# SwiGLU feed-forward on one core: gate and up of three chunks computed together, weights loaded once for three matmul pairs

## The chip, the core and the metric

The kernel runs on 1 core of one Trainium2 chip. The metric is the device time of one execution in microseconds (us), lower is better. A time before or after is the median of several runs. The profile comes from one execution by itself, whose own time is given beside its span.

## The reference

```python
def reference(x, w_gate, w_up, w_down):
    g = _silu(x @ w_gate)
    u = x @ w_up
    return (g * u) @ w_down
```

x is 1 x 2048 x 512, w_gate and w_up are 512 x 1376, w_down is 1376 x 512, all bfloat16. Two matrix products of the same input (gate and up), SiLU of the first, their product element by element, and a third matrix product (down).

## The kernel before, in words

The 2048 rows of x (tokens) are cut into 4 chunks of 512 (SC). The kernel holds x transposed (xT_sb: the 512 features on partitions, in 4 steps dk of 128), all weights, and the hidden values (hT_sb) in on-chip memory. A matmul takes a weight tile as its stationary operand (lhsT) and 512 tokens as its moving operand (rhs), and adds up the four steps dk in one of 8 banks of 128 x 512 float32.

**Groups.** One group is what fills one bank. The list `groups` fixes the order of PE's work and the bank of each group (number of the group modulo 8). For each chunk c and each of ten tiles ft of 128 hidden columns there is a group "G" (gate) and a group "U" (up), planned by `plan_pair`. 1376 is 10 x 128 + 96; the last 96 columns are handled apart: group "X" of a chunk (`plan_x`) holds the last 96 gate columns and the last 32 up columns, and group "Y" (`plan_y`) holds 64 further up columns for two chunks at once. The order is: for chunk 0 its ten G, U pairs, then X; the same for chunks 1, 2 and 3; then Y of chunks 0 and 1, Y of chunks 2 and 3. Then follow the groups "O" of the down product.

**Who reads a bank.** ACT (the scalar engine) computes SiLU of a G bank into one of NSG = 4 buffers sg_sb; DVE (the vector engine) multiplies it with the U bank into hT_sb. Of an X bank ACT takes two SiLUs (into sgx_sb and sgy_sb) and DVE one product (hx_sb). Of a Y bank DVE takes one product with sgy_sb (hy_sb). The operations stand in two lists, act_ops and dve_ops, in the order of planning, and each engine works its list in that order, waiting on semaphores: s_P counts finished groups, s_A and s_D the finished operations of ACT and DVE.

**What PE waits for.** Before a group's first matmul `free(g)` (L327) waits until all readers of the group eight places earlier, which had the same bank, are through. `gu_needs` (L348) waits for the loads: x of the chunk (x1, x2 or x3, for chunk 0 parts of its own) and the slab of weights. A load is waited for once. All waits are on PE's own instruction stream, so everything behind a wait waits too.

**Pairs.** From the fifth group on (`in_pairs`), `whole` (L334) issues each step dk as two matmuls of 64 weight columns each, at column 0 and column 64 of the array, writing the lower and the upper half of the same bank with the same moving operand. Each matmul brings its own weight load, which the profile shows as LDWEIGHTS on PEld.

**The loads.** SP issues nearly all DMAs in a written-out order (`loads_on_sync`, L124): parts of x of chunk 0 and the weights first, then the transposing loads x1, x2, x3 (L136, issued in L95), then w_down.

**The down product.** After the last Y group PE waits for all hT_sb. Then `strips` (L447) works in quads: four O groups at once, one for each chunk, each matmul using 32 rows of the array, with four row positions side by side (L470). The first pass works quad 0 and then quad 1, each over all ten tiles, before any other strip; `strips` calls `free` for all four groups of a quad before its first matmul. Quad 0 takes the banks of the groups eight to five places before the first O group, quad 1 those of the last four groups before it. In the kernel before, these last four are U of the last tile of chunk 3, X of chunk 3, and the two Y. The last four token tiles end with whole matmuls (L506). ACT and DVE copy the O banks to o_sb, and SP (one of the last by ACT) stores them.

Of the kernel before, what the change touches and what calls it, by code (L numbers as in the profile page):

```python
# [14 lines left out]
def bass_standalone__swiglu_ffn__prompt_kernel(nc, x, w_gate, w_up, w_down, out):  # L15
    _, S, D = x.shape
    F = w_gate.shape[1]
    P = 128
    KD = D // P
    NFF = F // P  # L20
    NFT = NFF + 1
    F_LAST = F - NFF * P
    SC = 512
    NSC = S // SC
# [5 lines left out]
    HT = SC // 2  # L30
    NXN = HT // P
    NB = 8
    NSG = 4
    NOS = 8
    SR = 32
    PW = 64
# [2 lines left out]
    Y_ROWS = [0, 64, 0, 64]  # L39
    X_ROWS = [64, 0, 96, 32]  # L40
    ORDER = [1, 2, 3, 0]
    assert D == 512 and S % SC == 0 and KD == 4 and F_LAST == 96 and NSC % 2 == 0

    xf = x[0]
# [3 lines left out]
    UPH = F + 32  # L48
    WTOT = 2 * F
    XC0 = NFF * P  # L50
    YC0 = UPH + NFF * P

    with ExitStack() as es:
# [7 lines left out]
        hT_sb = sb("hT_sb", [P, NFF, S], BF16)  # L61
# [3 lines left out]
        adummy = sb("act_dummy", [P, 8], FP32)  # L65
        sg_sb = [sb(f"sg_sb{i}", [P, SC], FP32) for i in range(NSG)]
        sgx_sb = [sb(f"sgx_sb{c}", [P, SC], FP32) for c in range(NSC)]
# [10 lines left out]
        s_P = sem("s_P")  # L78
# [70 lines left out]
        groups = []  # L149
# [3 lines left out]
        def add_group(kind, **what):  # L153
            g = dict(kind=kind, at=len(groups), bank=banks[len(groups) % NB], readers=[], **what)
            groups.append(g)
            return g

        def add_op(eng, g, **what):
            n_read[eng] += 1
            op = dict(g=g, at=n_read[eng], **what)  # L160
            (act_ops if eng == "A" else dve_ops).append(op)
            g["readers"].append((eng, op["at"]))
            return op

        def tview(i, dk):
            return banks[KD * i + dk][:, 0:P // 2].bitcast(BF16)

        sg_reader = []
        n_sg = 0
        h_ready = {}  # L170

        def plan_pair(c, ft):
            nonlocal n_sg
            gg = add_group("G", c=c, ft=ft)
            gu = add_group("U", c=c, ft=ft)
            b = n_sg % NSG
            free = sg_reader[n_sg - NSG] if n_sg >= NSG else 0
            a = add_op("A", gg, kind="silu", out=sg_sb[b][:, :], src=gg["bank"][:, :], free=free)
            d = add_op(
                "D", gu, kind="mul", out=hT_sb[:, ft, c * SC:(c + 1) * SC], a=sg_sb[b][:, :],  # L180
                b=gu["bank"][:, :], after=a["at"],
            )
            sg_reader.append(d["at"])
            h_ready[c] = d["at"]
            n_sg += 1

        def yblk(c):
            return (0, 64) if c % 2 == 0 else (64, 128)
# [4 lines left out]
        def plan_x(c):  # L193
            g = add_group("X", c=c)
            y0, y1 = yblk(c)
            add_op("A", g, kind="silu", out=sgx_sb[c][96:128, :], src=g["bank"][64:96, :], free=0)
            a = add_op("A", g, kind="silu", out=sgy_sb[c // 2][y0:y1, :], src=g["bank"][0:64, :], free=0)
            d = add_op(
                "D", g, kind="mul", out=hx_sb[X_ROWS[c]:X_ROWS[c] + SR, c, :],
                a=sgx_sb[c][96:128, :], b=g["bank"][96:128, :], after=a["at"] - 1,  # L200
            )
            y_after[c // 2] = a["at"]
            t_ready[c] = d["at"]
# [10 lines left out]
        for i in range(NXN):  # L214
            for dk in range(KD):
# [3 lines left out]
                    out=xT_sb[:, dk, i * P:(i + 1) * P], src=tview(i, dk), stored=(None, 0),  # L219
                )  # L220
                xt_ready[i, dk] = (eng, op["at"])

        for c in range(NSC):
            for ft in range(NFF):
                plan_pair(c, ft)
            plan_x(c)
        for pi in range(NSC // 2):
            plan_y(pi)
# [3 lines left out]
        n_store = [0] * NOS  # L232
        tiles = [c * TPC + q for q in range(TPC) for c in ORDER]
        for at, t in enumerate(tiles):
            ob = at % NOS
            if at == 2 * TPC:
                parted = add_op(
                    "D", dict(readers=[]), kind="copy", ready=(s_T, N_TURNS), out=part_sb[:, :],
                    src=banks[(NO + NST - 1) % NB][:, LASTH:D], stored=(None, 0),
# [4 lines left out]
            for c0, c1 in parts:  # L244
                g = add_group("O", t=t, c0=c0, c1=c1)
# [66 lines left out]
        def on_tensor(pe):  # L312
            landed = set()

            def need(name, count=1):
                if name not in landed:
                    pe.wait_ge(loads[name], 16 * count)
                    landed.add(name)
# [3 lines left out]
            def after(eng, n):  # L322
                if n > read[eng]:
                    pe.wait_ge(s_A if eng == "A" else s_D, n)
                    read[eng] = n

            def free(g):  # L327
                if g["at"] >= NB:
                    for eng, n in groups[g["at"] - NB]["readers"]:
                        after(eng, n)  # L330

            in_pairs = False

            def whole(bank, dk, col, c, n0, n1):  # L334
                if not in_pairs:
                    return pe.matmul(  # L336
                        bank[:, n0:n1], lhsT=w_sb[:, dk, col:col + P],
                        rhs=xT_sb[:, dk, c * SC + n0:c * SC + n1], start=(dk == 0), stop=(dk == KD - 1),
                    )
                for y0 in (0, PW):  # L340
                    ins = pe.matmul(  # L341
                        bank[y0:y0 + PW, n0:n1], lhsT=w_sb[:, dk, col + y0:col + y0 + PW],
                        rhs=xT_sb[:, dk, c * SC + n0:c * SC + n1], start=(dk == 0), stop=(dk == KD - 1),
                        tile_position=(0, y0), skip_group_check=True,
                    )
                return ins

            def gu_needs(g, n0, n1):  # L348
                c, ft = g["c"], g["ft"]
                if c > 0:  # L350
                    need(f"x{c}")
                if c == 0 and n1 > HT:
                    need("x0b")
                if c == 0 and n1 > HT + P:
                    need("x0c")
                need(("wg" if g["kind"] == "G" else "wu") + str(slab_of[ft]))

            def gu_step(g, dk, n0, n1):
                c = g["c"]
                col = (0 if g["kind"] == "G" else UPH) + g["ft"] * P  # L360
                if c == 0:
                    for i in range(n0 // P, min(n1 // P, NXN)):
                        after(*xt_ready[i, dk])
                ins = whole(g["bank"], dk, col, c, n0, n1)
                if n1 == SC and dk == KD - 1:
                    ins.then_inc(s_P, 1)

            def gu_matmuls(g, n0, n1):
                if g["c"] == 0:
                    for i in range(n0 // P, min(n1 // P, NXN)):  # L370
                        after(*xt_ready[i, 0])
                gu_needs(g, n0, n1)
                for dk in range(KD):
                    gu_step(g, dk, n0, n1)
# [38 lines left out]
                gu_matmuls(g, HT, SC)  # L413

            for g in groups[NB:NO]:
                free(g)
                kind = g["kind"]
                if kind in "GU":
                    gu_matmuls(g, 0, SC)
                elif kind == "X":  # L420
                    c = g["c"]
                    need(f"wg{slab_of[NFF]}")
                    need("wut")
                    for dk in range(KD):
                        ins = whole(g["bank"], dk, XC0, c, 0, SC)
                    ins.then_inc(s_P, 1)
                elif kind == "Y":
                    need(f"wu{slab_of[NFF]}")
                    for dk in range(KD):
                        for c in (2 * g["pi"], 2 * g["pi"] + 1):  # L430
                            y0, y1 = yblk(c)
                            ins = pe.matmul(  # L432
                                g["bank"][y0:y1, :], lhsT=w_sb[:, dk, YC0:YC0 + 64],
                                rhs=xT_sb[:, dk, c * SC:(c + 1) * SC],
                                start=(dk == 0), stop=(dk == KD - 1),
                                tile_position=(0, y0), skip_group_check=True,
                            )
                    ins.then_inc(s_P, 1)
# [8 lines left out]
            def strips(q, k, fks, start, stop, turn=True):  # L447
# [7 lines left out]
                for fk in fks:  # L455
                    if fk == NFF:
                        need("wdt", 2 + TPC)
                    for c, g in zip(ORDER, quad):
                        t = g["t"]
# [38 lines left out]
            for g in groups[NO + TPC * (TPC - 1):]:  # L498
# [6 lines left out]
                for fk in full[1:]:  # L505
                    ins = pe.matmul(  # L506
                        g["bank"][:, 0:c1 - c0], lhsT=hT_sb[:, fk, t * P:(t + 1) * P],
                        rhs=wd_sb[:, fk, c0:c1], start=(rest and fk == 1), stop=(fk == NFF - 1),
                        skip_group_check=True,
                    )  # L510
# [3 lines left out]
        on_gpsimd(nc.gpsimd)  # L514
        on_scalar(nc.scalar)
        on_tensor(nc.tensor)
        on_vector(nc.vector)

# [27 lines left out]
```

## Time and profile before

| | |
|---|---|
| time, median of 3 runs | 120.16 us |
| the runs | 119.78 to 120.52 us |
| the profiled execution's own time | 120.42 us |
| its span, first to last instruction | 119.1 us |
| PE busy | 116.2 us, 98% |
| PE weight loads (PEld) busy | 63.5 us, 1386 loads |
| DVE busy / ACT busy | 38.8 us / 35.1 us |
| granted TensorE clock | 1.000 |

How to read it: PE is the matmul engine, PEld its weight loads, which can run beside a matmul, and SP the queue that issues most DMAs. A group of instructions in the profile is named by line, engine and operation, "out<-in" by the program's tile names and the shapes (partitions x elements), then the count, the busy time in us and the mean duration of one in ns, then the idle time of the engine just before them and what ended it. A row of the timeline gives start and length in us, then the engine, the line and the merged instructions with their count. Matmuls of one engine overlap in part: a matmul's own duration is longer than the time from its start to the start of the next, so the rate is read from a row of many.

### The profile page before, as it was taken

What the parts mean: (1) busy time and instruction counts of PE and PEld (TensorE: products, weight loads), DVE (VectorE), ACT (ScalarE), POOL (GpSimd) and SP (SyncE); (2) the same over time, 40 slices, a digit from 0 to 9 for tenths busy, and PEclk for the clock granted to TensorE, in tenths of its full rate; (3) what the DMA queues carried; (4) which work ended last, traced back from release to release, by engine and by line L of the source; (5) the groups of instructions that cost most, each with busy time, mean ns of one, the idle gap of its engine ahead of it and who ended that gap; (6) DMA issues with size and microseconds to landing.
All of it is one profiled execution on the core that took longest, in us unless ns stands there. A gap on an engine that the chain in (4) does not pass through costs nothing.

```text
span 119.1 us, 3076 instructions
## 1 busy us (share of the span) xinstructions
PE 116.2 (98%) x1385; PEld 63.5 (53%) x1386; DVE 38.8 (33%) x62; ACT 35.1 (29%) x62; POOL 0.5 (0%) x5
## 2 busy tenths in 40 slices
PE   7999999999999999999999999999999999999993
PEld 2999555555555555555555555544444444444463
DVE  0204634444334444344353344361000044004322
ACT  3406443262442363432454423430000033002121
POOL 1000000000000000000000000000000000000000
DMA  4999989995000000000000000000000015300522
GB/s 92 281 197 336 262 175 99 263 331 155 6 0 0 0 6 0 0 3 3 6 0 0 0 0 6 0 0 0 6 0 6 0 47 196 115 6 0 194 76 88
DMA packets 17533, 8.78 MB, mean 74 GB/s; under 512 B 10608, under 2 KB 17520, under 8 KB 17520
## 3 DMA queue, kind: packets, MB, share of 16 engines
q1 hardware_dynamic: 16704, 8.23, 28.9%
q10 hardware_dynamic: 816, 0.36, 1.1%
q8 instruction: 11, 0.18, 0.6%
q14 instruction: 2, 0.02, 0.0%
HBM read 4.65 MB, written 2.10 MB: 57 GB/s over the span
## 4 chain that ended last, share of the span: by engine, by line
PE 98%; issue 0%; DVE 0%
PE bank L341 60%; PE bank L470 25%; PE bank L506 7%; PE bank L378 2%; PE bank L336 2%; PE bank L432 1%; PE bank L388 1%; DVE o_sb L307 0%
## 5 line engine op out<-in xcount | busy, mean ns | idle before, releaser
L341 PE MATMUL bank<-xT_sb,w_sb 128*64 128x512 bf16 (+2 forms) x720 | 71.1, 360 | 0.0
L341 PEld LDWEIGHTS bank<-xT_sb,w_sb 128*64 128x64 bf16 x720 | 39.6, 110 | 31.2 <-issue 0.2
L302 DVE TENSOR_TENSOR hT_sb<-sg_sb,bank 128x512 bf16<-128x512 f32 x40 | 27.5, 688 | 40.6 <-PE bank L341 39.7
L294 ACT ACTIVATE sg_sb<-bank 128x512 f32<-128x512 f32 x40 | 23.8, 596 | 41.0 <-PE bank L341 40.9
L470 PE MATMUL bank<-wd_sb,hT_sb 32*128 32x512 bf16 x496 | 28.8, 374 | 0.0
L470 PEld LDWEIGHTS bank<-wd_sb,hT_sb 32*128 32x128 bf16 x496 | 12.7, 93 | 14.2 <-issue 0.4
L294 ACT ACTIVATE o_sb<-bank 128x512 bf16<-128x512 f32 (+1 forms) x8 | 4.2, 568 | 33.0 <-PE bank L470 27.8
L309 DVE CAST o_sb<-bank 128x512 bf16<-128x512 f32 x8 | 5.3, 688 | 21.2 <-PE bank L470 17.3
L506 PE MATMUL bank<-wd_sb,hT_sb 128*128 128x512 bf16 (+3 forms) x62 | 7.8, 286 | 0.2 <-issue 0.2
L506 PEld LDWEIGHTS bank<-wd_sb,hT_sb 128*128 128x128 bf16 x63 | 4.6, 98 | 3.7 <-issue 0.4
L470 PE MATMUL bank<-wd_sb,hy_sb 32*128 32x512 bf16 x32 | 4.6, 374 | 0.0
L378 PE MATMUL bank<-const-bfloat16-1.0 128*128 128x128 bf16 (+1 forms) x11 | 3.1, 455 | 0.8 <-PEq L531 0.8
L302 DVE TENSOR_TENSOR hx_sb<-sgx_sb,bank 32x512 bf16<-32x512 f32 x4 | 2.8, 692 | 3.5 <-ACT sgx_sb L294 3.5
L294 ACT ACTIVATE sgx_sb<-bank 32x512 f32<-32x512 f32 x4 | 2.4, 588 | 4.5 <-PE bank L341 4.5
L309 DVE COPY part_sb<-bank 128x256 f32<-128x256 f32 x1 | 0.4, 426 | 8.2 <-PE bank L470 8.2
L470 PE MATMUL bank<-wd_sb,hx_sb 32*128 32x512 bf16 x16 | 3.0, 374 | 0.0
L336 PE MATMUL bank<-xT_sb,w_sb 128*128 128x128 bf16 (+1 forms) x24 | 2.9, 294 | 0.0
L378 PEld LDWEIGHTS bank<-const-bfloat16-1.0 128*128 128x128 bf16 x11 | 1.4, 143 | 2.2 <-issue 2.2
L336 PEld LDWEIGHTS bank<-xT_sb,w_sb 128*128 128x128 bf16 x24 | 2.5, 130 | 0.1
L294 ACT ACTIVATE sgy_sb<-bank 64x512 f32<-64x512 f32 x4 | 2.4, 589 | 0.1
L309 DVE COPY xT_sb<-bank 128x128 bf16<-128x128 bf16 x4 | 0.9, 224 | 4.3 <-PE bank L388 4.3
L432 PE MATMUL bank<-xT_sb,w_sb 128*64 128x512 bf16 x16 | 1.9, 379 | 0.0
(15 smaller groups left out, 10.1 us busy)
## 6 DMA issues: line engine op xcount, KB each, us to landing
out_dram<-o_sb SPq DMA_DIRECT2D x15, 128.0 KB, 1.8
wd_sb<-in_w_down_dram SPq DMA_DIRECT2D x1, 1280.0 KB, 7.6
w_sb<-in_w_gate_dram SPq DMA_DIRECT2D x1, 480.0 KB, 5.5
w_sb<-in_w_up_dram SPq DMA_DIRECT2D x1, 448.0 KB, 7.5
w_sb<-in_w_gate_dram SPq DMA_DIRECT2D x1, 384.0 KB, 4.2
w_sb<-in_w_up_dram SPq DMA_DIRECT2D x1, 384.0 KB, 4.6
w_sb<-in_w_up_dram SPq DMA_DIRECT2D x2, 128.0 KB, 3.2
w_sb<-in_w_gate_dram SPq DMA_DIRECT2D x1, 256.0 KB, 3.7
```

Source lines behind the costliest of these rows:

```text
L294: act.activation(op["out"], op["src"], fn).then_inc(s_A, 1)
L302: ins = dve.tensor_tensor(op["out"], op["a"], op["b"], ALU.mult)
L309: ins = dve.tensor_copy(op["out"], op["src"])
L336: return pe.matmul(bank[:, n0:n1], lhsT=w_sb[:, dk, col:col + P], rhs=xT_sb[:, dk, c * SC + n0:c * SC + n1], start=(dk == 0), stop=(dk == ...
L341: ins = pe.matmul(bank[y0:y0 + PW, n0:n1], lhsT=w_sb[:, dk, col + y0:col + y0 + PW], rhs=xT_sb[:, dk, c * SC + n0:c * SC + n1], start=(dk ...
L378: pe.matmul(banks[NB - 1][:, 0:width], lhsT=ones_w, rhs=ones_m[:, 0:width], start=True, stop=True)
L388: ins = pe.matmul(tview(i, dk)[y0:y0 + width, :], lhsT=xn_sb[:, i, dk * P + y0:dk * P + y0 + width], rhs=ident[:, :], start=True, stop=Tru ...
L432: ins = pe.matmul(g["bank"][y0:y1, :], lhsT=w_sb[:, dk, YC0:YC0 + 64], rhs=xT_sb[:, dk, c * SC:(c + 1) * SC], start=(dk == 0), stop=(dk == ...
L470: ins = pe.matmul(g["bank"][:, :], lhsT=h, rhs=wd_sb[r0:r0 + SR, w, :], start=(start and fk == fks[0]), stop=(stop and fk == fks[-1]), til ...
L506: ins = pe.matmul(g["bank"][:, 0:c1 - c0], lhsT=hT_sb[:, fk, t * P:(t + 1) * P], rhs=wd_sb[:, fk, c0:c1], start=(rest and fk == 1), stop=( ...
```

## The change

Chunk 0 stays as it is, with its X group behind it. For chunks 1, 2 and 3 the order changes: for each tile ft the three G groups stand together, then the three U groups; after the ten tiles the three X groups stand together, and then the two Y groups as before. Inside such a set of three groups the loop goes over the step dk outside and the three chunks inside: the first chunk's pair of matmuls is issued with its weight loads, and the pairs of the other two chunks with `ldweights=False` (`held_matmul`), so that they use the weights that are in the array. Before a set PE waits for the banks of all three groups and for the loads of all three chunks. The buffers of SiLU grow from 4 to 6. Loads, their order, and the down product are not changed. The last four groups ahead of the down product are now X of chunk 2, X of chunk 3 and the two Y, and the four before them U of the last tile of chunks 1, 2, 3 and X of chunk 1.

```diff
--- before.py
+++ after.py
@@ -30,7 +30,7 @@
     HT = SC // 2
     NXN = HT // P
     NB = 8
-    NSG = 4
+    NSG = 6
     NOS = 8
     SR = 32
     PW = 64
@@ -39,6 +39,7 @@
     Y_ROWS = [0, 64, 0, 64]
     X_ROWS = [64, 0, 96, 32]
     ORDER = [1, 2, 3, 0]
+    HELD = [1, 2, 3]
     assert D == 512 and S % SC == 0 and KD == 4 and F_LAST == 96 and NSC % 2 == 0
 
     xf = x[0]
@@ -169,20 +170,21 @@
         n_sg = 0
         h_ready = {}
 
-        def plan_pair(c, ft):
+        def plan_set(cs, ft):
             nonlocal n_sg
-            gg = add_group("G", c=c, ft=ft)
-            gu = add_group("U", c=c, ft=ft)
-            b = n_sg % NSG
-            free = sg_reader[n_sg - NSG] if n_sg >= NSG else 0
-            a = add_op("A", gg, kind="silu", out=sg_sb[b][:, :], src=gg["bank"][:, :], free=free)
-            d = add_op(
-                "D", gu, kind="mul", out=hT_sb[:, ft, c * SC:(c + 1) * SC], a=sg_sb[b][:, :],
-                b=gu["bank"][:, :], after=a["at"],
-            )
-            sg_reader.append(d["at"])
-            h_ready[c] = d["at"]
-            n_sg += 1
+            ggs = [add_group("G", c=c, ft=ft) for c in cs]
+            gus = [add_group("U", c=c, ft=ft) for c in cs]
+            for c, gg, gu in zip(cs, ggs, gus):
+                b = n_sg % NSG
+                free = sg_reader[n_sg - NSG] if n_sg >= NSG else 0
+                a = add_op("A", gg, kind="silu", out=sg_sb[b][:, :], src=gg["bank"][:, :], free=free)
+                d = add_op(
+                    "D", gu, kind="mul", out=hT_sb[:, ft, c * SC:(c + 1) * SC], a=sg_sb[b][:, :],
+                    b=gu["bank"][:, :], after=a["at"],
+                )
+                sg_reader.append(d["at"])
+                h_ready[c] = d["at"]
+                n_sg += 1
 
         def yblk(c):
             return (0, 64) if c % 2 == 0 else (64, 128)
@@ -220,9 +222,12 @@
                 )
                 xt_ready[i, dk] = (eng, op["at"])
 
-        for c in range(NSC):
-            for ft in range(NFF):
-                plan_pair(c, ft)
+        for ft in range(NFF):
+            plan_set([0], ft)
+        plan_x(0)
+        for ft in range(NFF):
+            plan_set(HELD, ft)
+        for c in HELD:
             plan_x(c)
         for pi in range(NSC // 2):
             plan_y(pi)
@@ -331,14 +336,23 @@
 
             in_pairs = False
 
-            def whole(bank, dk, col, c, n0, n1):
+            def held_matmul(out, lhsT, rhs, start, stop, tile_position=(0, 0), skip_group_check=False):
+                ins = mybir.InstMatmult(
+                    name=nc.get_next_instruction_name(), engine=mybir.EngineType.PE, ldweights=False,
+                    start_tensor_calc=start, stop_tensor_calc=stop, ins=[pe.lower_ap(rhs), pe.lower_ap(lhsT)],
+                    outs=[pe.lower_ap(out)], tile_position=tile_position, tile_size=(P, lhsT.shape[1]),
+                )
+                return pe.add_instruction(ins)
+
+            def whole(bank, dk, col, c, n0, n1, held=False):
+                matmul = held_matmul if held else pe.matmul
                 if not in_pairs:
-                    return pe.matmul(
+                    return matmul(
                         bank[:, n0:n1], lhsT=w_sb[:, dk, col:col + P],
                         rhs=xT_sb[:, dk, c * SC + n0:c * SC + n1], start=(dk == 0), stop=(dk == KD - 1),
                     )
                 for y0 in (0, PW):
-                    ins = pe.matmul(
+                    ins = matmul(
                         bank[y0:y0 + PW, n0:n1], lhsT=w_sb[:, dk, col + y0:col + y0 + PW],
                         rhs=xT_sb[:, dk, c * SC + n0:c * SC + n1], start=(dk == 0), stop=(dk == KD - 1),
                         tile_position=(0, y0), skip_group_check=True,
@@ -413,8 +427,26 @@
                 gu_matmuls(g, HT, SC)
 
             for g in groups[NB:NO]:
+                kind = g["kind"]
+                if g.get("c", 0) > 0:
+                    if g["c"] != HELD[0]:
+                        continue
+                    together = groups[g["at"]:g["at"] + len(HELD)]
+                    for h in together:
+                        free(h)
+                    if kind != "X":
+                        for h in together:
+                            gu_needs(h, 0, SC)
+                        col = (0 if kind == "G" else UPH) + g["ft"] * P
+                    else:
+                        col = XC0
+                    for dk in range(KD):
+                        for h in together:
+                            ins = whole(h["bank"], dk, col, h["c"], 0, SC, held=h is not g)
+                            if dk == KD - 1:
+                                ins.then_inc(s_P, 1)
+                    continue
                 free(g)
-                kind = g["kind"]
                 if kind in "GU":
                     gu_matmuls(g, 0, SC)
                 elif kind == "X":
```

## Prediction before the run

> **What bounds the kernel now.** I read the page first: the busy times, then the groups of instructions.
>
> ```profile
> span 119.1 us, 3076 instructions
> ## 1 busy us (share of the span) xinstructions
> PE 116.2 (98%) x1385; PEld 63.5 (53%) x1386; DVE 38.8 (33%) x62; ACT 35.1 (29%) x62; POOL 0.5 (0%) x5
> ```
>
> PE is busy 98% of the span, and there is one weight load for each matmul. The chain of waits, in order of time, names PE alone from 0.84 us to the last multiplication, but for gaps of 0.16 us and less:
>
> ```profile
> 0.84 2.61 PE bank L378 x8
> ...
> 7.12 70.99 PE bank L341 x720
> 78.11 1.73 PE bank L432 x16
> 79.84 29.46 PE bank L470 x544
> 109.30 0.16 issue
> 109.46 7.80 PE bank L506 x62
> 117.26 0.02 issue
> 117.28 0.22 DVE o_sb L307
> ```
>
> The stage that the change edits is L341. The groups kept apart by shape say what a matmul and a load last there, and three looks at the timeline say how fast they follow each other:
>
> ```profile
> L341 PE MATMUL bank<-xT_sb,w_sb 128*64 128x512 bf16 x608 | 65.8, 379 | 0.0
> L341 PEld LDWEIGHTS bank<-xT_sb,w_sb 128*64 128x64 bf16 x720 | 39.6, 110 | 31.2 <-issue 0.2
> ```
>
> ```profile
> 23.77 53.48 PE L341 MATMUL bank<-xT_sb,w_sb 128*64 128x512 bf16 x494
> ```
>
> ```profile
> 6.19 0.93 PE L336 MATMUL bank<-xT_sb,w_sb 128*128 128x256 bf16 x7
> ```
>
> ```profile
> 109.46 5.78 PE L506 MATMUL bank<-wd_sb,hT_sb 128*128 128x512 bf16 x26 [0.16 <-issue]
> ```
>
> The first row is 247 pairs without a gap, so a pair takes (53.48 - 0.38) / 246 = 0.216 us. A single 128-column matmul with one load (third row) takes (5.78 - 0.38) / 25 = 0.216 us as well. Half the stream (second row, 256 elements) takes (0.93 - 0.27) / 6 = 0.110 us. Twice that is 0.220, so at most some 3.5 ns (2 to 5, the row being rounded) of a 216 ns slot do not grow with the length of the stream. The slot is the streaming of 512 elements, and nothing else fills it. Where the load lies is seen in a narrow window:
>
> ```profile
> 39.96 0.60 PE L341 MATMUL bank<-xT_sb,w_sb 128*64 128x512 bf16 x4
> 40.17 0.60 ACT L294 ACTIVATE sg_sb<-bank 128x512 f32<-128x512 f32 x1 [1.13 <-PE bank L341]
> 40.17 0.11 PEld L341 LDWEIGHTS bank<-xT_sb,w_sb 128*64 128x64 bf16 x2
> ```
>
> Both loads of the next pair begin with the running pair, at 40.17, lie side by side, and are over after 0.11 us; the pair takes 0.216. The loads are hidden twice over.
>
> **The change part by part.**
>
> *Loads removed.* In the sets of chunks 1 to 3 there are 21 sets (10 gate, 10 up, 1 tail) of 4 steps, hence 84 changes of weights instead of 252. 168 pairs are issued without loads, and 336 of the 1386 loads go. They lie wholly under the stream, so I cost their removal at nothing. The bounds: the part of the slot that does not grow with the stream could be the price of changing weights; then each held pair saves up to 3.5 ns, 168 x 3.5 ns = 0.6 us. I take 0, because the slot is 0.216 us with one load of 128 columns (L506) and with two of 64 (L341): the number of loads does not show in it.
>
> *The 84 loads that stay.* Each must still be hidden, now behind the third, held pair. The trace has no held matmul, so I bound it by the one place where this form of load was not hidden:
>
> ```profile
> 6.74 0.38 PE L336 MATMUL bank<-xT_sb,w_sb 128*128 128x256 bf16 x2
> 7.04 0.36 PEld L341 LDWEIGHTS bank<-xT_sb,w_sb 128*64 128x64 bf16 x8 [0.21 <-issue]
> 7.05 0.52 PE L341 MATMUL bank<-xT_sb,w_sb 128*64 128x256 bf16 x6
> ```
>
> Three pairs here last 0.52 us where 2 x 0.110 + 0.27 = 0.49 is due: 0.03 us of load shows. The last matmul before starts at 6.74 + 0.11 = 6.85, so the first pair is also late, by 7.05 - 6.85 - 0.11 = 0.09 us, part of which is the change from 128 to 64 columns. So a load that is not hidden costs 0.03 to 0.12 us, 84 times 2.5 to 10 us. I take 0: the load in program order stands directly behind the last held pair, and in the narrow window loads already start with the pair before them. The gain of the other end is the 0.6 us above.
>
> [...]
>
> *The order of the work: x3.* Each set now waits for the loads of chunks 1, 2 and 3 before its first matmul; before, chunk 3 was not needed until two chunks later. PE stands in line for it, with everything else behind.
>
> ```profile
> 18.08 3.52 SPq L95 DMA_TRANSPOSE xT_sb<-in_x_dram  x1
> ```
>
> ```profile
> xT_sb<-in_x_dram SPq DMA_TRANSPOSE x2, 6.1
> ```
>
> ```profile
> 23.76 0.59 ACT L294 ACTIVATE sgx_sb<-bank 32x512 f32<-32x512 f32 x1 [1.13 <-PE bank L341]
> 24.38 0.59 ACT L294 ACTIVATE sgy_sb<-bank 64x512 f32<-64x512 f32 x1
> 24.87 0.58 ACT L294 ACTIVATE sg_sb<-bank 128x512 f32<-128x512 f32 x1
> ```
>
> The first row is the issue of x3, the second (DMA issues between 18 and 21 us) gives 6.1 us to landing for x2 and x3: x3 lands near 24.1. The third fence is the end of chunk 0. In the quoted rows of the tail below, the SiLU of the last group starts 78.15 - 77.94 = 0.21 us after the first matmul of the next, so the first set could start at 23.76 - 0.21 = 23.55. PE waits 0.55 us. The ends: 0.3 if it lands a little earlier in other executions, 0.8 with the 0.21 us of idle that the first load at 7.04 shows on top. The DMAs themselves, and their order on SP's queue, are not changed, so nothing moves them.
>
> *Banks and buffers inside the sets.* A set lasts 12 x 0.216 = 2.59 us and holds three banks; its first group is done 9 slots + 0.43 (0.21 and a slot) = 2.37 us after its start. An up set must find the first group of the up set before it multiplied: that ends 2.37 - 2.59 + 0.69 = 0.47 us after the gate set between them begins, 2.1 us before it is wanted. A gate set needs the last two multiplications of an earlier up set, which end by 1.9 us into the gate set before: 3.3 us to spare. ACT has 3 x 0.60 and DVE 3 x 0.69 us of work in 5.18. Six buffers of SiLU cover a full round. Cost nothing; it would cost only if a reader took over 2 us longer.
>
> *The tail.* Before, one X group stood ahead of the two Y groups; now three do, and finish within two slots of each other. The timeline around it:
>
> ```profile
> 77.94 1.89 PE L432 MATMUL bank<-xT_sb,w_sb 128*64 128x512 bf16 x16
> 78.15 0.59 ACT L294 ACTIVATE sgx_sb<-bank 32x512 f32<-32x512 f32 x1 [1.13 <-PE bank L341]
> 78.76 0.59 ACT L294 ACTIVATE sgy_sb<-bank 64x512 f32<-64x512 f32 x1
> 78.84 0.69 DVE L302 TENSOR_TENSOR hx_sb<-sgx_sb,bank 32x512 bf16<-32x512 f32 x1 [0.86 <-ACT sgx_sb L294]
> 79.56 1.28 DVE L302 TENSOR_TENSOR hy_sb<-sgy_sb,bank 128x512 bf16<-128x512 f32 x2
> 79.77 6.65 PE L470 MATMUL bank<-wd_sb,hT_sb 32*128 32x512 bf16 x120
> ```
>
> Call 77.94, the first Y matmul, E. The second quad of L470 reuses the banks of the last four groups, Y1 among them. It starts ten slots and some 0.01 us after 79.77, at E + 4.00; Y1's multiplication ends at 79.56 + 1.28 = E + 2.90. That is 1.10 us of slack. Now ACT has six SiLUs in a row. The first can start at E + 0.21 - 2 x 0.216 = E - 0.22, and they follow each other in 0.61 us (78.15 to 78.76): the fifth (X of chunk 3) starts at E + 2.22 and ends at 2.81, DVE multiplies it 0.10 later (78.74 to 78.84) at 2.91, Y0 starts 0.72 behind (78.84 to 79.56) at 3.63, and the two Y end 1.28 later at E + 4.91. The slack of 1.10 becomes a stall of 0.91, and with 0.04 to wake PE (an estimate: less than half of the 0.10 in which DVE follows ACT above), 0.95. The ends: 0.7 if ACT goes from one bank to the next in 0.49 (24.38 to 24.87), twice; 1.15 with the 0.21 of idle of the first load at 7.04. The first quad needs only X1 among the late ones (its multiplication ends near E + 1.2, and it starts at E + 1.83). What is late next: nothing, the strips after it use results that are then ready.
>
> **Sum.** 0 + 0 + 0.55 + 0 + 0.95 = +1.5 us. The profiled execution took 120.42 us, of which 119.1 are the span, so it would become 121.9. It stands 0.26 above the median of the runs, 120.16, to which I refer the forecast: 121.7 us.
>
> **The rivals.**
> 1. *The remaining loads are not hidden.* PE may need the held pair to be over before it takes new weights. For: no row shows a held matmul. Against: loads start with the running pair. It gives 2.5 to 10 us on top: 124.2 us, at worst about 132.
> 2. *A pair without loads is a little shorter.* 0.6 us off: 121.1 us, 0.8% up. For: the part that does not grow with the stream. Against: it is the same with one and with two loads.
> 3. *The x3 wait is hidden anyway*, because the transpose lands before 23.55 in most executions. Against: 0.5 us is far for a landing to move. 120.16 + 0.95 = 121.1 us.
> 4. *The other side: loads take time from the stream.* Place: every slot. If each load slows the pair under which it lies, holding repays; it decides once a held pair saves more than 1.5 us / 168 = 9 ns. At the 0.03 us of the shown load, 168 x 0.03 = 5.0 us: 116.7; at the full 0.11, 18.5 us: 103.2. Against it: the 0.220 of twice the short slot leaves 5 ns at most.
>
> **How the numbers follow.** Forecast (both stalls, pairs at 0.216): 0.58, of which 0.10 falls below +1%, since with both stalls at their low ends the sum is 1.0. Rival 1: 0.19, of which 0.12 near 124.2 and 0.07 far above. Rival 2: 0.10. Rival 3: 0.08. Rival 4: 0.05. About 1% is what a measurement of this kernel can tell from no change. Slower by over 1% (above 121.36): 0.48 + 0.19 = 0.67. Within 1%: 0.10 + 0.10 + 0.08 = 0.28. Faster: 0.05. The range runs from 120.7, which is low stalls (1.0) with most of rival 2 (0.5), to 124.2, which takes in the low end of rival 1; rival 4 and the upper end of rival 1 stay outside, 0.12 together.
>
> **What would show it.** Right: 1050 weight loads; matmul pairs in the sets still 0.216 us apart; one idle time of PE near 23.6 us, of about half a microsecond, that ends with x3; one of about 0.95 near 83 us, released by DVE's hy_sb; and L470 and L506 as long as before. Wrong: a slot of 0.213 or less in held pairs (rival 2 or 4), a late pair every third slot (rival 1), PE idle inside the sets (my cover of banks), or no idle near 23.6 (rival 3).

## The result, and the profile after

The changed kernel takes 121.74 us (median of 6 runs, 121.69 to 122.08) against 120.31 us for the kernel before (6 runs, 119.78 to 120.52, the three ahead of the prediction among them): a ratio of 1.013, 95% interval 1.0107 to 1.0152. It is 1.4 us slower. The profiled execution took 121.73 us.

The head of its page, with the loads that went (1386 to 1050):

```profile
span 120.5 us, 2759 instructions
...
PE 116.7 (97%) x1385; PEld 46.5 (39%) x1050; DVE 37.0 (31%) x62; ACT 33.1 (28%) x62; POOL 0.5 (0%) x5
```

PE's busy time rose by 0.5 us and the span by 1.4; the rest is PE standing still. The waits of the matmul engine show where. They stand as who waited for whom, then the total, the number of times and the longest, in us:

```profile
PE bank L502 <- DVE hy_sb L307: 0.9, 1, 0.9
PE bank L392 <- PEq L563: 0.8, 1, 0.8
...
PE bank L538 <- issue: 0.2, 1, 0.2
```

The last two were there before; the first is new. The chain of waits, which before ran through PE from end to end but for one step of DVE at the close, now leaves PE here: it passes through six SiLUs of ACT, from 78.02 us on, and then through DVE:

```profile
81.89 1.30 DVE hy_sb L307 x2
83.32 27.38 PE bank L502 x504
```

And the timeline of the tail, PE, ACT and DVE; this is the view to lay beside the last fence of the prediction's cost part:

```profile
78.02 0.59 ACT L299 ACTIVATE sgx_sb<-bank 32x512 f32<-32x512 f32 x1 [3.60 <-PE bank L355]
...
78.25 1.89 PE L464 MATMUL bank<-xT_sb,w_sb 128*64 128x512 bf16 x16
...
80.47 0.59 ACT L299 ACTIVATE sgx_sb<-bank 32x512 f32<-32x512 f32 x1
81.08 0.59 ACT L299 ACTIVATE sgy_sb<-bank 64x512 f32<-64x512 f32 x1
81.16 0.69 DVE L307 TENSOR_TENSOR hx_sb<-sgx_sb,bank 32x512 bf16<-32x512 f32 x1 [0.53 <-ACT sgx_sb L299]
81.89 1.29 DVE L307 TENSOR_TENSOR hy_sb<-sgy_sb,bank 128x512 bf16<-128x512 f32 x2
...
83.32 1.04 PE L502 MATMUL bank<-wd_sb,hT_sb 32*128 32x512 bf16 x16 [0.91 <-DVE hy_sb L307]
```

With E = 78.25 the last product of a Y bank ends at 83.18 = E + 4.93, and the second quad starts at E + 5.07 instead of E + 4.00: 1.07 us lost. (The 0.91 of the row is less by 0.16: a matmul of L502 lasts 0.374 us, and the next four start 0.216 us after the last four.)

Inside the sets nothing changed. The busy times by stretch, first of the kernel before and then of the changed one (columns: stretch, its length, then busy us and count of PE, PEld, DVE, ACT, POOL, then granted clock, DMA share, GB/s):

```profile
40.00:50.00 10.00, 10.00 (x96) 5.29 (x94) 4.13 (x6) 4.50 (x8) 0.00 (x0) 1.00 0.01 2
60.00:70.00 10.00, 10.00 (x96) 5.25 (x94) 4.14 (x6) 4.53 (x8) 0.00 (x0) 1.00 0.00 0
```

```profile
40.00:50.00 10.00, 10.00 (x96) 1.71 (x30) 3.40 (x6) 3.15 (x6) 0.00 (x0) 1.00 0.00 0
60.00:70.00 10.00, 10.00 (x96) 1.72 (x32) 3.66 (x6) 3.15 (x6) 0.00 (x0) 1.00 0.01 2
```

A third of the loads, and the same 96 matmuls in the same 10 us.

At the other place, the start of the first set, the changed kernel did not wait. The timeline of PE there:

```profile
23.64 0.60 PE L355 MATMUL bank<-xT_sb,w_sb 128*64 128x512 bf16 x4
24.07 0.60 PE L345 MATMUL bank<-xT_sb,w_sb 128*64 128x512 bf16 x4
24.50 0.38 PE L355 MATMUL bank<-xT_sb,w_sb 128*64 128x512 bf16 x2
```

The rows follow each other in slots of 0.216 us (held pairs are L345). In this execution x3 landed at 23.0 us and chunk 0 ended at 23.86; in the profile before, x3 landed at 24.0. SP needed less time here to issue the three loads x1, x2 and x3, as its queue shows, first before and then after:

```profile
9.82 11.78 SPq L95 DMA_TRANSPOSE xT_sb<-in_x_dram  x3
```

```profile
9.89 11.06 SPq L96 DMA_TRANSPOSE xT_sb<-in_x_dram  x3
```

What is left of the difference lies at the very start. The first 64-column pair stands at 7.05 us before (the row is in the prediction) and here at

```profile
7.35 0.52 PE L355 MATMUL bank<-xT_sb,w_sb 128*64 128x256 bf16 x6
```

So of the 1.40 us between the two profiled executions' spans (119.07 and 120.47 with one more digit), 0.30 are spent before any changed instruction of PE and 1.09 from there to the last matmul: 1.07 in the tail wait and 0.02 in quads that then start less evenly.

### The profile page after: what moved, and what is told of

Read it like the earlier page. It is cut to its first block, busy times and chain, and to the rows that moved or that the text cites. A ratio compares the mean times of both kernels' runs of the same rounds, so it can differ in the third digit from the quotient of the medians.

```text
span 120.5 us, 2759 instructions
## 1 busy us (share of the span) xinstructions
PE 116.7 (97%) x1385; PEld 46.5 (39%) x1050; DVE 37.0 (31%) x62; ACT 33.1 (28%) x62; POOL 0.5 (0%) x5
## 4 chain that ended last, share of the span: by engine, by line
PE 93%; ACT 3%; DVE 1%; issue 1%; DVEq 0%
PE bank L345 30%; PE bank L355 29%; PE bank L502 23%; PE bank L538 6%; PE bank L392 2%; PE bank L350 2%; ACT sgy_sb L299 1%; ACT sgx_sb L299 1%; DVE hy_sb L307 1%; PE bank L402 1%; DVE o_sb L312 0%; DVEq L306 0%
## 5 line engine op out<-in xcount | busy, mean ns | idle before, releaser
L345 PE MATMUL bank<-xT_sb,w_sb 128*64 128x512 bf16 x336 | 50.3, 379 | 0.0
L355 PE MATMUL bank<-xT_sb,w_sb 128*64 128x512 bf16 (+2 forms) x384 | 48.6, 344 | 0.0
L355 PEld LDWEIGHTS bank<-xT_sb,w_sb 128*64 128x64 bf16 x384 | 20.6, 110 | 49.7 <-issue 44.5
L307 DVE TENSOR_TENSOR hT_sb<-sg_sb,bank 128x512 bf16<-128x512 f32 x40 | 25.7, 684 | 44.9 <-PE bank L355 44.5
L299 ACT ACTIVATE sg_sb<-bank 128x512 f32<-128x512 f32 x40 | 21.7, 598 | 45.0 <-PE bank L355 44.9
L502 PE MATMUL bank<-wd_sb,hT_sb 32*128 32x512 bf16 x496 | 29.1, 374 | 0.9 <-DVE hy_sb L307 0.9
L502 PEld LDWEIGHTS bank<-wd_sb,hT_sb 32*128 32x128 bf16 x496 | 14.3, 93 | 13.6 <-issue 1.8
L502 PE MATMUL bank<-wd_sb,hy_sb 32*128 32x512 bf16 x32 | 4.7, 374 | 0.0
L502 PE MATMUL bank<-wd_sb,hx_sb 32*128 32x512 bf16 x16 | 3.1, 374 | 0.0
```

The lines of the kernel that those rows point to most:

```text
L299: act.activation(op["out"], op["src"], fn).then_inc(s_A, 1)
L307: ins = dve.tensor_tensor(op["out"], op["a"], op["b"], ALU.mult)
L345: return pe.add_instruction(ins)
L355: ins = matmul(bank[y0:y0 + PW, n0:n1], lhsT=w_sb[:, dk, col + y0:col + y0 + PW], rhs=xT_sb[:, dk, c * SC + n0:c * SC + n1], start=(dk == ...
L502: ins = pe.matmul(g["bank"][:, :], lhsT=h, rhs=wd_sb[r0:r0 + SR, w, :], start=(start and fk == fks[0]), stop=(stop and fk == fks[-1]), til ...
```

## The experiments

Two theories stood against each other. A: the order alone costs the time, by waits at its two ends, and holding weights is worth nothing because a load was hidden already. B: holding saves something that the order eats up, or held pairs cost something. All kernels are measured against the kernel before on the same chip.

**all_loaded.** The new order, but no pair held:

```diff
-    ins = whole(h["bank"], dk, col, h["c"], 0, SC, held=h is not g)
+    ins = whole(h["bank"], dk, col, h["c"], 0, SC, held=False)
```

> The order of the change, but every pair with its own weight loads (1386 loads instead of 1050). Theory A, the order alone costs the time and holding is worth nothing: the same as the changed kernel, before + 1.4 us, pairs 0.216 us apart, PE idle 1.07 us ahead of the second quad. Rival B, holding saves time that the order eats up: slower than the changed kernel by 0.3 us or more (before + 1.7 and above). Rival C, held pairs or the reload behind them cost something that the profile does not show: faster than the changed kernel by 0.3 us or more (before + 1.1 and below).

Measured: 121.44 us, before 120.08, ratio 1.0113 (1.0079 to 1.0147). Its waits and matmuls:

```profile
PE bank L502 <- DVE hy_sb L307: 0.9, 1, 0.9
```

```profile
L355 PE MATMUL bank<-xT_sb,w_sb 128*64 128x512 bf16 x608 | 65.8, 379 | 0.0
```

The busy time of 65.8 us for 608 matmuls is that of the kernel before to the digit. The times agree with the changed kernel's, but their interval is some 0.4 us wide on each side; the sharper reading is in the traces. From the first 64-column pair to the last matmul's start the changed kernel takes 111.10 us and this one 111.09. The two agree to 0.01 us, and what difference there is does not favour holding: 168 held pairs save nothing. Theory B is out.

**x_before_last_tile, first_tile_apart, both.** The first takes away the tail wait, the second puts the need for x3 off by 3.5 us, the third does both:

```diff
 for ft in range(NFF):
+    if ft == NFF - 1:
+        for c in HELD:
+            plan_x(c)
     plan_set(HELD, ft)
-for c in HELD:
-    plan_x(c)
```

```diff
-    plan_set(HELD, ft)
+    for cs in ([[c] for c in HELD] if ft == 0 else [HELD]):
+        plan_set(cs, ft)
...
-    if g["c"] != HELD[0]:
+    apart = kind != "X" and g["ft"] == 0
+    if g["c"] != HELD[0] and not apart:
         continue
-    together = groups[g["at"]:g["at"] + len(HELD)]
+    together = groups[g["at"]:g["at"] + (1 if apart else len(HELD))]
```

> The changed kernel with the set of the three X groups moved ahead of the last tile's gate and up sets, so that their readers are done long before the down product. Theory A, the tail wait is the chain of six SiLUs and the products behind it: the idle of 1.07 us ahead of the second quad goes; about 0.1 us comes back ahead of the first quad, which now waits for the last product of chunk 3 (some 0.05 us past the moment at which PE gets there); the time is before + 0.4 to 0.5 us. Rival, the idle belongs to the change of array use or to w_down: it stays, before + 1.4.

> The changed kernel, but the first tile of chunks 1 to 3 goes chunk by chunk (each pair with its loads), so that x of chunk 3 is needed 3.5 us later, after it has landed (23.0 and 24.0 us in the two profiles so far). If the wait for x3 costs 0.36 us in a usual execution, which is what the changed kernel's 1.43 us leave beside the tail wait of 1.07: before + 1.05 us. If the wait is hidden in most executions and the rest comes from the start of the kernel: before + 1.4 us, as the changed kernel.

> Both edits in the changed kernel: X ahead of the last tile, and the first tile chunk by chunk. Theory A (two waits, holding worth nothing): before + 0 to 0.15 us, the 0.1 us being the small new wait ahead of the first quad. If something else in the order costs time steadily: before + 0.4. If holding saves 3.5 ns a pair, 150 held pairs: before - 0.4.

Measured: 120.54 us, ratio 1.0031 (1.0009 to 1.0053); 121.37 us, ratio 1.0096 (1.0065 to 1.0126); 120.53 us, ratio 1.0036 (1.0014 to 1.0058); before 120.08 us for all three. The tail of x_before_last_tile:

```profile
77.45 1.88 DVE L308 TENSOR_TENSOR hT_sb<-sg_sb,bank 128x512 bf16<-128x512 f32 x3 [1.35 <-PE bank L356]
...
77.67 1.89 PE L465 MATMUL bank<-xT_sb,w_sb 128*64 128x512 bf16 x16
...
79.25 1.28 DVE L308 TENSOR_TENSOR hy_sb<-sgy_sb,bank 128x512 bf16<-128x512 f32 x2
...
79.65 1.04 PE L503 MATMUL bank<-wd_sb,hT_sb 32*128 32x512 bf16 x16
```

The products of the two Y banks now end at 79.25 + 1.28 = 80.53, 1.3 us before the second quad wants their banks, and the wait for hy_sb is gone. The first quad starts at E + 1.98 instead of E + 1.83: 0.15 us where 0.1 was expected. The third product of hT_sb, for which it now has to wait, ends at 79.33, 0.32 us before it; behind hy_sb PE had started after 0.14 us (83.18 to 83.32), so this small delay is only in part explained. The tail wait is the chain that the prediction drew, shown by taking it away: from first pair to last matmul 110.16 us, against 111.10.

first_tile_apart takes 111.10 from pair to end, like the changed kernel: it removed no wait, because in the profiles of the changed order there was none. The two experiments agree with that: putting off x3 alone (first_tile_apart) or on top (both) moved nothing beyond their intervals. The miss in my expectations is that both still lies 0.4 us above the kernel before, where its trace accounts for 0.15. That is the number of its second alternative, a steady cost of something else in the order.

**before_again, after_again.** The same two kernels as entries of their own, to see how much of that is chance.

> The kernel before, unchanged, as a second entry. From the first 64-column pair to the last matmul the profiles so far take 110.01 us for the kernel before and 111.09 for every kernel with the new order and the late X set, to 0.01 us; the first such pair starts anywhere from 6.54 to 7.35 us. If the start is chance, this kernel gives 110.01 us again, a ratio of 1.000 with an interval that says how far medians wander, and a first pair anywhere from 6.5 to 7.4. If the start of the new order is later by itself, the first pair stands at or below 6.8 here.

> The changed kernel again, beside the kernel before on the same chip. If the start is chance: 111.09 us from the first pair to the last matmul and before + 1.1 us, with an interval that takes in 1.009. If the new order has a steady loss beyond the tail wait: before + 1.4 again. If x3 lands after the end of chunk 0 in this execution (24.0 us as in the first profile of the kernel before), PE idles between them, and the 111.09 grow by that much.

Measured: before_again 120.13 us against 120.31 for itself, ratio 0.9985 (0.9965 to 1.0006); after_again 121.66 us, ratio 1.0113 (1.0087 to 1.0139). Read from the start times in the eight traces:

| kernel | first 64-column pair at, us | from there to the last matmul, us |
|---|---|---|
| before / before_again | 7.05 / 6.82 | 110.01 / 110.01 |
| changed / after_again | 7.35 / 7.33 | 111.10 / 111.10 |
| all_loaded | 6.54 | 111.09 |
| first_tile_apart | 7.07 | 111.10 |
| x_before_last_tile | 6.78 | 110.16 |
| both | 7.10 | 110.16 |

The second column repeats to 0.01 us for each order; the first wanders over 0.8 us for matmuls that are the same in all kernels. One cause shows in the same 20 matmuls of the start, here of the changed kernel and of all_loaded:

```profile
4.85 2.57 PE L350 MATMUL bank<-xT_sb,w_sb 128*128 128x128 bf16 x20
```

```profile
4.81 1.80 PE L350 MATMUL bank<-xT_sb,w_sb 128*128 128x128 bf16 x20
```

They start alike and last 0.77 us longer in the one: the change to a quicker pace comes later. The matmuls of 128 elements start 0.107 us apart at first and 0.056 us apart later (those of 256: 0.21 and 0.11). The change from one pace to the other comes near 6.6 us in the changed kernel and near 4.7 us in all_loaded; over the eight traces it lies between 3.6 and 6.7 us. The granted clock reads 1.00 in all eight, from 0 to 7.0 us and from 7.0 to 12.5 us; what sets the moment was not shown. A second cause shows in two of the eight, before_again and first_tile_apart. Their chains of waits lead back from the first pair to the load of a slab of gate weights:

```profile
2.82 3.95 DMA w_sb<-in_w_gate_dram
```

```profile
2.82 4.20 DMA w_sb<-in_w_gate_dram
```

It lands at 6.77 and at 7.02 us, and the first pair starts 0.05 us behind it, at 6.82 and 7.07, although the quicker pace was there by 3.6 and 5.5 us. So in these two it was the load that set the start.

1.09 us of 120.3 is a ratio of 1.009. after_again's interval takes it in, the first measurement's (from 1.0107) does not quite. By the medians all six entries of the new order lie 0.20 to 0.34 us above what their traces account for, while the same kernel entered twice differs by 0.2 us. So the traces speak for a start that varies by chance, and the times, all six on one side, for a small steady cost. The wait for x3 is not it, since the kernels that put x3 off show the same. Whether a few tenths of a microsecond belong to the change stays open.

**x3_last.** Does the first set really stand in line for chunk 3? The load of x3 goes behind w_down:

```diff
-    for c in range(1, NSC):
+    for c in range(1, NSC - 1):
         load_x(sp, f"x{c}", c * SC, (c + 1) * SC)
...
+    load_x(sp, "x3", 3 * SC, S)
```

> The changed kernel with the load of x3 moved behind w_down on SP's queue. Its issue starts near 22.6 us (w_down's seven issues take 4.5 us from 18.1), so with 6 us to landing it lands near 29. If the first set stands in line for chunk 3, PE idles from 23.6 us until then, some 5 to 6 us, and the time is before + 6.5 to 7.5; the granted clock may fall behind so long an idle, which would add to it. If the wait is only needed at chunk 3's own pair and the two others go ahead, PE works on for a step's two pairs (0.4 us) first. If x3 were not waited for there: before + 1.4.

Measured: 129.03 us (2 runs), before 120.31, ratio 1.0728 (1.0692 to 1.0765). PE's timeline and the stretches around the wait:

```profile
21.66 2.11 PE L356 MATMUL bank<-xT_sb,w_sb 128*64 128x512 bf16 x18
28.70 0.64 PE L356 MATMUL bank<-xT_sb,w_sb 128*64 128x512 bf16 x2 [4.93 <-DMA xT_sb<-in_x_dram]
29.10 1.09 PE L346 MATMUL bank<-xT_sb,w_sb 128*64 128x512 bf16 x4
```

```profile
29.00:33.00 4.00, 4.00 (x22) 0.63 (x6) 0.00 (x0) 0.00 (x0) 0.00 (x0) 0.50 0.00 0
34.00:40.00 6.00, 6.00 (x60) 1.25 (x20) 1.88 (x3) 2.20 (x5) 0.00 (x0) 1.00 0.00 0
```

The wait is real and it holds the whole set: nothing of chunks 1 and 2 is issued before chunk 3 has landed. The idle costs 5.1 us in matmul starts. Behind the 4.93 us of idle the granted clock is 0.50 until some 4.7 us after PE goes on (28.70 to 33.4), 22 matmuls in 4 us where later 60 go in 6: about 2.3 us more. Together 7.4 us: 118.53 from first pair to last matmul, against 111.10. The time is before + 8.7, over the 6.5 to 7.5 of the expectation, which had put no figure on the clock.

**pieces128_loaded, pieces64_loaded, pieces64_held.** When would holding pay? The sets' moving operands are cut into shorter pieces, with and without holding (here for pieces of 64, every pair with its loads):

```diff
-    for dk in range(KD):
-        for h in together:
-            ins = whole(h["bank"], dk, col, h["c"], 0, SC, held=h is not g)
+    for n0 in range(0, SC, 64):
+        for dk in range(KD):
+            for h in together:
+                ins = whole(h["bank"], dk, col, h["c"], n0, n0 + 64, held=False)
...
```

> Where would holding pay? The sets of the changed kernel with their moving operand cut into pieces of 128 tokens (each piece goes through its four steps before the next one begins), every pair with its loads: 1008 pairs of 128 instead of 252 of 512. Chunk 0 has such pairs, with loads, 56 ns apart. Theory A, a load runs under the pair before it and is not seen: 1008 x 56 ns = 56.4 us instead of 54.4, the time is before + 1.1 + 2.0 = 3.1 us. Rival, two loads of 110 ns occupy the array one after the other where they come in a row: pairs 110 ns apart, before + 58 us.

> The same in pieces of 64 tokens, every pair with its loads: 2016 pairs. The whole matmuls of the last tiles go 29 ns apart at 64 elements with a load of 128 columns each. Theory A for pairs: 29 ns again, 58.5 us, before + 5.2 us. If a load of 64 columns keeps its half of the array busy longer than the stream of 64 (it was measured at 110 ns from start to end), the pair spacing is the load's: 55 ns gives before + 57 us, 110 ns before + 168 us.

> Pieces of 64 tokens with the weights held for the second and third chunk: 672 pairs with loads, 1344 held. If loads do not show at 64 (29 ns with loads): the same time as with all loads, before + 5.2 us. If a loaded pair costs 55 ns and a held one 29: before + 23 us, some 35 us less than with all loads; here holding would pay. If the spacing is set by the issue of two matmuls and not by loads: both alike, whatever the spacing.

Measured, 2 runs each, before 120.35 us: 125.20 us, ratio 1.0403 (1.0207 to 1.0599); 180.62 us, ratio 1.5007 (1.4866 to 1.5148); 142.71 us, ratio 1.1858 (1.1465 to 1.2251). The first is before + 4.9, nearer to Theory A (3.1) than to its rival (58), but 1.8 over it: its trace has two pauses put down to "issue" (0.8 us) and a tail wait of 1.2 us instead of 0.9, and the rest was not followed up. The last two, before + 60.3 and + 22.4, come near the numbers of the second alternative (57 and 23), 55 ns for a loaded pair and 29 for a held one, yet the profile shows that the reason behind them is wrong. The waits of PE in the two kernels of 64, with all loads first:

```profile
PEld bank L355 <- issue: 44.7, 29, 3.3
PE bank L355 <- issue: 41.5, 29, 3.1
```

```profile
PEld bank L355 <- issue: 13.7, 22, 1.1
PE bank L355 <- issue: 5.4, 10, 0.9
PE bank L345 <- issue: 5.0, 10, 0.9
```

"issue" means that the engine waited for nothing that the profile shows, and the idle comes in pauses of up to 3.1 us. Between the pauses loaded pairs run fast, here 64 of them in one burst of pieces64_loaded:

```profile
41.13 2.21 PE L355 MATMUL bank<-xT_sb,w_sb 128*64 128x64 bf16 x128 [1.12 <-issue]
```

(2.21 - 0.20) / 63 = 0.032 us a pair, with two loads in it. Held and loaded together (next rows, pieces64_held) make three pairs in 0.09 us, 0.030 each:

```profile
30.20 0.20 PE L355 MATMUL bank<-xT_sb,w_sb 128*64 128x64 bf16 x2
30.23 0.23 PE L345 MATMUL bank<-xT_sb,w_sb 128*64 128x64 bf16 x4
30.29 0.20 PE L355 MATMUL bank<-xT_sb,w_sb 128*64 128x64 bf16 x2
```

So even at 64 tokens the loads are nearly hidden, 0.032 us against 0.030. What the two kernels have alike is the time for one instruction. In the stretch from 24 to 80 us, all loads first, then held:

```profile
24.00:80.00 56.00, 36.32 (x1983) 34.69 (x1975) 10.11 (x16) 8.62 (x17) 0.00 (x0) 0.94 0.09 27
```

```profile
24.00:80.00 56.00, 48.20 (x3044) 46.02 (x1014) 13.90 (x23) 13.22 (x26) 0.00 (x0) 1.00 0.07 21
```

1983 + 1975 = 3958 instructions, and 3044 + 1014 = 4058, both in 56 us: 14.1 and 13.8 ns for each instruction of PE, loads counted alike. The granted clock of 0.94 in the first row is not the reason: from 40 to 60 us, at 1.00 in both, it is 14.3 and 13.5 ns. Holding helps there by 38 us, which is what its fewer instructions come to: 2688 loads less, at 14 ns each, are 38 us. In the kernel of this case a pair with its loads is 4 instructions in 216 ns, 54 ns for each, far from that.

The pauses come at a fixed distance. In both kernels they stand 255 or 256 instructions of PE apart, with one exception (the burst of 64 pairs above is one such stretch: 128 matmuls and their 128 loads). The page of a kernel counts, among its DMA queues, one of the kind "instruction"; for pieces64_loaded, as number, MB and share:

```profile
q8 instruction: 38, 0.62, 1.4%
```

That is 16 KB for each transfer. There are 28 of them in pieces64_held and 9 in the changed kernel. Every pause of more than 0.15 us in the sets (29 in the first trace, 20 in the second) ends 1.2 to 1.6 us after such a transfer has ended. I read this as PE waiting for its own instructions; no run changed their supply, so the cause itself was not shown.

## Why the prediction was right, and where not

The forecast was 121.7 us, within 120.7 to 124.2, and slower by over 1% at 0.67; 121.74 came out. The sum came out right in part by luck: of its two terms the tail was larger, the wait for x3 was absent, and some 0.36 us that it did not contain stood in its place.

- *Loads removed, 0.* Right, and exactly: pairs 0.216 us apart in both, 168 held pairs worth nothing to 0.01 us (all_loaded). The 3.5 ns that do not grow with the stream are not the price of changing weights.
- *The loads that stay, 0.* Right: no late pair at any third slot. Rivals 1, 2 and 4 are out.
- *The order, x3, 0.55 us.* This step failed. It took the landing near 24.1 us and chunk 0's end at 23.55 from one execution as if both were fixed, and held against rival 3 that 0.5 us is far for a landing to move. x3 landed between 22.6 and 24.7 us in the eight traces with the loads in their order, a spread of 2.1 us; in three of them (both of the kernel before, and first_tile_apart) this is 0.5 to 1.1 us after chunk 0's end, in the five others 0.2 to 0.9 before it. In none of the four of them in which the first set waits for x3 did it cost anything: rival 3. The place is right (x3_last); the price depends on when x3 lands, which moved by more than the whole term from one execution to the next.
- *Banks inside the sets, 0.* Right, no idle there.
- *The tail, 0.95 us.* Right in mechanism, 0.12 too small: 1.07. The chain fits step by step (third product of X starts at E + 2.91 as forecast; Y0 at 3.63, measured 3.64; end at 4.91, measured 4.93); PE's start behind it took 0.14 us, not the 0.04 that I set.
- *What made up the missing 0.4 us.* Without x3 the sum is 1.07, and 1.43 was measured. In the two profiles 0.30 of the difference is the start of the kernel, whose matmuls are the same in both and whose length differs by up to 0.8 us between executions. Why the new order's times lie 0.20 to 0.34 us high in all six entries stays open. The forecast owes this part to luck.

## What to carry to other kernels

In this kernel a weight load that started with the pair before it and was over after 0.11 of the pair's 0.216 us cost nothing, so removing 336 of them gained nothing (111.10 us from first pair to last matmul, 111.09 with all of them); look at the slot, not at the busy time of the loads. Holding weights gained 38 us in the kernel of 64-token pieces, whose trace has pauses put down to "issue", with one exception 255 or 256 instructions apart: many short matmuls with such pauses are where it is worth trying. And when groups of work are put side by side, draw the chain of readers at the end of the set: here three groups that finished within two slots handed a queue of six SiLUs to the next stage, and the second quad, which needed a bank behind the last of them, started 1.07 us late.

## What the runs showed of the hardware that I had not expected

- Over 56 us PE took one instruction in 14.1 ns in pieces64_loaded and in 13.8 ns in pieces64_held, in bursts of 255 or 256 (with one exception) and with pauses of up to 3.1 us between them. Each pause of more than 0.15 us in the sets ended 1.2 to 1.6 us after a 16 KB transfer on the queue of the kind "instruction".
- A load of 64 columns lasted 110 ns from start to end in the kernel before and 115 in pieces64_loaded, but in a burst of the latter, pairs with two such loads ran 32 ns apart: loads overlapped each other, and the duration of one was no bound for the pace of many.
- The moment at which the matmuls of the start change to the quicker pace (those of 128 elements from 0.107 to 0.056 us apart) differs from execution to execution, from 3.6 to 6.7 us in the eight traces. Together with the landing of a slab of weights it moves the first pair, and everything after, by 0.8 us, about as much as the six times of the kernel before are apart.
